# Subtracting the lower halves of the gathered expert rows on GpSimd instead of VectorE

## The chip, the cores and the metric

The kernel runs on one core of one Trainium2 chip. The metric is the device time of one launch in microseconds (us), the median of several executions. A core has a matrix engine (TensorE; PE in the profile, PEld for its weight loads), a vector engine (VectorE; DVE), an activation engine (ScalarE; ACT), GpSimd (POOL) and SyncE (SP). Each engine takes its own instructions strictly in the order in which they were written to it, and a semaphore makes an instruction wait for one of another engine or for a transfer.

## What is computed

Attention over 8 batches of 576 tokens and 8 heads, half of the heads with a local mask and half with a strided one, and then a mixture of 8 experts, each of which takes 576 of the 4608 tokens. The second half, in which the change lies, is this:

```python
def _moe_ref(x, w_gate, w1, w2):          # x: 4608 x 512, w1: 8 x 512 x 1024, w2: 8 x 1024 x 512
    logits = x @ w_gate
    ...                                    # tokens are assigned in order of their logits, 576 to an expert
    for e in range(E):
        mask = assigned == e
        h = np.maximum(x[mask] @ w1[e], 0.0)
        out[mask] = h @ w2[e]
    return out.astype(np.float32)
```

All matrices are float32. The kernel reaches that accuracy with float16 matmuls: every operand is split into an upper half (the value rounded to float16) and a lower half (value minus upper half, rounded to float16), and three of the four products are added.

## The kernel before

The attention part fills the first 200 us or so and writes the rows of x to a buffer in DRAM, `x_scr`. The experts then follow in eight rounds, numbered 0 to 7 here as `ph` is in the code. A round closes one expert. What a round does for its expert lies ahead of that expert's matmuls, beside the matmuls of the expert before it:

- A search (`search`, lines L833 to L871) finds by counting which logit is the limit for the 576 best tokens. It is a loop of VectorE, TensorE, VectorE, TensorE: `cm` (L833) compares, a matmul (L849) counts, `red` and `r` (L852, L855) reduce, a matmul (L858) sums, `g` (L865) decides, a matmul (L868) spreads it. These small matmuls stand between the large ones in TensorE's queue.
- `indices` gives the list of the expert's tokens, `idx`.
- `tokens` gathers these rows from `x_scr` with five indirect transfers issued by GpSimd (L1089, tiles `xr`; four of 128 rows and one of 64).
- `halve` turns each of the five pieces into float16 halves: ScalarE copies the upper half into `xg` (L1078), VectorE subtracts for the lower half (L1079), and SyncE issues a transposing transfer from `xg` to `xt` (L1080). There are four `xg` buffers, so that the fifth piece waits for the transpose of the first.
- `weights` loads w1 and w2 of the expert and splits them: ScalarE squares (L1011) for a scale and writes the upper halves `w1h` and `w2h` (L1029), VectorE makes the lower halves `w1l` and `w2l` (L1030).
- `ffn` does the matmuls, first the 1024 hidden rows (`hidden`, L1180, which read `xt`, `w1h` and `w1l`), then the output (L1222 for the last 64 tokens, L1228 for the others). ScalarE scales an output tile into `y` (L1238), and GpSimd scatters it with an indirect transfer (L1239).

In round 0 three of the five pieces go another way (`turn`, on TensorE), so that `halve` runs 2 + 7 x 5 = 37 times. The order of each engine is fixed when the program is built: the code above gives due times to the steps of loading, searching and halving (`T_ROWS`, `T_ROW` and others), and a priority (`urgent`) lets a step go ahead of the others on its engine. On GpSimd the experts' part holds almost nothing but the gathers and the scatters, which in each round of the middle come as five gathers and then five scatters. The matmuls of line L1180 read all 576 columns of `xt` from the second matmul on, since each weight tile meets columns 0 to 287 and then columns 288 to 575.

Of the kernel before, what the change touches and what calls it, by code (L numbers as in the profile page):

```python
# [13 lines left out]
OP = mybir.AluOpType  # L14
# [121 lines left out]
def band_stride_attention_then_capacity_moe(ctx, tc, qt, kl, ks, nl, ns, wg, w1, w2, cst, out, dbg=None):  # L136
    nc = tc.nc
# [615 lines left out]
    def urgent(ph=1):  # L753
        return tc.high_priority(offset=URGENT * (2 if ph == 0 else 1))
# [319 lines left out]
    def halve(ph, xt, xr, t, n):  # L1074
        xg = xp.tile([128, 2 * DM], F16, name="xg", bufs=4)
        xs, xv = xg[:n].rearrange("q (a j d) -> q j a d", a=2, j=2), xr[:n].rearrange("q (a d) -> q a d", a=2)
        with urgent(ph):
            nc.scalar.activation(xs[:, 0], xv, AF.Copy)  # L1078
            nc.vector.tensor_tensor(xs[:, 1], xv, xs[:, 0], op=OP.subtract)  # L1079
            nc.sync.dma_start_transpose(xt[:, :, t * 128:t * 128 + n], xg[:n])  # L1080

    def tokens(ph, idx):
        xt = xp.tile([128, 2 * 2 * 2, CAP], F16, name="xt")
        todo = []
        for t in range(NT):
            n = min(128, CAP - 128 * t)
            xr = xp.tile([128, DM], F32, name="xr", bufs=5)
            with urgent(ph):
                nc.gpsimd.indirect_dma_start(out=xr[:n], out_offset=None, in_=x_rows,  # L1089
                                             in_offset=bass.IndirectOffsetOnAxis(ap=idx[:n, t:t + 1], axis=0))  # L1090
            if ph or t >= TURNS:
                todo.append(lambda t=t, n=n, xr=xr: halve(ph, xt, xr, t, n))
            else:
                todo.append(lambda t=t, n=n, xr=xr: turn(xt, xr, t, n))
        return xt.rearrange("p (a j d) n -> p a j d n", a=2, j=2), todo
# [256 lines left out]
```

## Time and profile before

| | |
|---|---|
| median of three executions | 700.05 us (698.74 to 703.6) |
| the profiled execution | 699.79 us, its span 698.0 us |
| busy, share of the span | PE 88%, PEld 58%, DVE 66%, ACT 50%, POOL 16% |
| mean granted TensorE clock | 0.943 |
| L1079 on DVE | 37 instructions, 25.3 us in all, 689 ns mean |
| L1089 and L1239 on POOL | 40 and 40 instructions, 41.4 us and 48.2 us in all |

The profile is of one execution. Its span runs from the first instruction to the last, and about 1.8 us of the execution's time lie around it. A row of the timeline gives start, duration, engine, line, operation, output<-inputs, and in square brackets how long the engine had idled and what ended that; the start times count from the start of the span. A row of the waits names who waited, for whom, the sum in us, how many times, and the longest. A row of the chain gives a piece of the sequence of work that ended last, each step led back to what released it.

### The profile page before, as it was taken

Reading aid. Unit: us, or ns where it says so; the run is one execution under the profiler, and the core shown is the slowest. Engines: PE = TensorE matmul, PEld = TensorE weight load, DVE = VectorE, ACT = ScalarE, POOL = GpSimd, SP = SyncE. Lnnn points to the kernel's source line nnn. Section 1 sums busy time; section 2 is a strip of 40 time slices with the busy share of each in tenths; the row PEclk is TensorE's granted clock in tenths of the full one; section 3 lists DMA queues with packets and bytes.
Section 4 is the critical chain, followed back from the end, with each engine's and each line's share of the span. In section 5 each row is a group of like instructions: output and inputs, shape, how many; then the busy total and the mean of one; then the engine's idle time right before and its main releaser. Section 6 shows DMA issues by size and latency. Waiting matters only on the chain.

```text
span 698.0 us, 19758 instructions
## 1 busy us (share of the span) xinstructions
PE 614.9 (88%) x8289; PEld 407.6 (58%) x8289; DVE 460.3 (66%) x1388; ACT 348.6 (50%) x567; POOL 109.4 (16%) x124
## 2 busy tenths in 40 slices
PE   7699998989984488989989989999998998999993
PEld 4476776757764266458547547647645744755741
DVE  3767777767847778786777777778767666681200
ACT  2655754565420456582573464384375277871210
POOL 2101110111000200330240050051041032211011
PEclk9989999989975699999999999999999999999997
DMA  8958888777120630860770670491385089731010
GB/s 235 260 164 237 237 238 237 197 214 208 38 70 2 242 91 1 294 151 2 267 179 1 234 197 16 164 249 34 104 252 92 2 297 267 212 62 54 1 39 31
DMA packets 76364, 102.42 MB, mean 147 GB/s; under 512 B 41292, under 2 KB 49062, under 8 KB 75763
## 3 DMA queue, kind: packets, MB, share of 16 engines
q1 hardware_dynamic: 68195, 79.61, 40.0%
q0 software_dynamic: 7360, 21.15, 9.9%
q8 instruction: 65, 1.06, 0.7%
q10 hardware_dynamic: 720, 0.39, 0.2%
q14 instruction: 24, 0.20, 0.1%
HBM read 73.60 MB, written 18.87 MB: 132 GB/s over the span
## 4 chain that ended last, share of the span: by engine, by line
PE 20%; issue 13%; DMA 11%; DVE 10%; ACT 5%; POOL 3%; SPq 1%; POOLq 0%; ACTq 0%
PE ph L1180 16%; DMA w<-in_w_dram 6%; DMA xt<-xg 2%; DMA xr<-x_scr,idx 2%; POOL xr L1089 2%; DVE w1l L1030 2%; POOL out_dram L1239 1%; ACT jk L1011 1%; PE ph L1228 1%; DVE w2l L1030 1%; SPq L996 1%; ACT w1h L1029 1%; DVE hl L1188 1%; DVE xg L1079 1%; ACT hh L1187 1%
## 5 line engine op out<-in xcount | busy, mean ns | idle before, releaser
L1180 PE MATMUL ph<-xt,w1h 128*128 128x288 f16 (+2 forms) x1024 | 177.7, 289 | 6.2 <-DMA xt<-xg 5.1
L1180 PEld LDWEIGHTS <-w1h 128*128 128x128 f16 x1024 | 97.6, 99 | 37.6 <-issue 7.0
L1180 PE MATMUL ph<-xt,w1l 128*128 128x288 f16 (+2 forms) x512 | 111.5, 289 | 0.0
L1239 POOL DMA_INDIRECT out_dram<-y,idx x40 | 48.2, 1204 | 337.0 <-ACT y L1238 308.1
L1011 ACT ACTIVATE jk<-w 128x1024 f16<-128x1024 f32 x64 | 67.4, 1054 | 64.6 <-DMA w<-in_w_dram 63.6
L1187 ACT ACTIVATE hh<-ph 128x576 f16<-128x576 f32 (+2 forms) x72 | 42.7, 594 | 110.9 <-PE ph L1180 110.7
L1228 PE MATMUL ph<-w2h,hl 128*128 128x512 f16 x256 | 97.5, 381 | 0.0
L1228 PE MATMUL ph<-w2h,hh 128*128 128x512 f16 x256 | 97.3, 380 | 0.1
L1228 PE MATMUL ph<-w2l,hh 128*128 128x512 f16 x256 | 97.4, 380 | 0.0
L1228 PEld LDWEIGHTS <-hh 128*128 128x128 f16 x512 | 49.2, 98 | 57.9 <-issue 7.7
L1188 DVE SCALAR_TENSOR_TENSOR hl<-ph,hh 128x576 f16<-128x576 f32 (+2 forms) x72 | 49.5, 687 | 46.6 <-ACT hh L1187 46.6
L1180 PEld LDWEIGHTS <-w1l 128*128 128x128 f16 x512 | 50.5, 99 | 13.5 <-issue 0.6
L1089 POOL DMA_INDIRECT xr<-x_scr,idx x40 | 41.4, 1034 | 52.5 <-DMA w<-in_w_dram 25.5
L371 ACT ACTIVATE pr<-spa 128x576 f32<-128x576 f32 x32 | 20.8, 650 | 56.5 <-PE spa L368 45.6
L1030 DVE SCALAR_TENSOR_TENSOR w1l<-w,w_sw,w1h 128x512 f16<-128x512 f32 x64 | 45.4, 744 | 4.9 <-ACT w1h L1029 4.8
L1228 PEld LDWEIGHTS <-hl 128*128 128x128 f16 x256 | 25.0, 98 | 39.6 <-issue 14.8
L1030 DVE SCALAR_TENSOR_TENSOR w2l<-w,w_sw,w2h 128x512 f16<-128x512 f32 x64 | 46.3, 742 | 1.8 <-ACT w2h L1029 1.3
L1238 ACT ACTIVATE y<-ph,so 128x512 f32<-128x512 f32 x32 | 21.7, 680 | 45.7 <-PE ph L1228 31.8
L1029 ACT ACTIVATE w2h<-w,w_sw 128x512 f16<-128x512 f32 x64 | 41.2, 711 | 5.4 <-DVE w_sw L206 5.4
L1029 ACT ACTIVATE w1h<-w,w_sw 128x512 f16<-128x512 f32 x64 | 42.1, 708 | 3.0 <-DVE w_sw L206 1.8
L422 POOL DMA_DIRECT2D x_scr<-xs x23 | 15.0, 657 | 173.3 <-DVE xs L406 124.9
L1079 DVE TENSOR_TENSOR xg<-xr,xg 128x512 f16<-128x512 f32 (+1 forms) x37 | 25.3, 689 | 16.0 <-ACT xg L1078 15.7
(610 smaller groups left out, 973.9 us busy)
## 6 DMA issues: line engine op xcount, KB each, us to landing
w<-in_w_dram SPq DMA_DIRECT2D x64, 512.0 KB
kl<-in_kl_dram SPq DMA_DIRECT2D x16, 304.0 KB
v_s<-in_ns_dram SPq DMA_DIRECT2D x16, 292.5 KB
v_l<-in_nl_dram SPq DMA_DIRECT2D x16, 292.5 KB
ks<-in_ks_dram SPq DMA_DIRECT2D x16, 288.0 KB
qs<-in_qt_dram SPq DMA_DIRECT2D x16, 288.0 KB
ql<-in_qt_dram SPq DMA_DIRECT2D x16, 288.0 KB
x_scr<-xl SPq DMA_DIRECT2D x8, 512.0 KB
```

What stands on the lines that cost most here:

```text
L371: nc.scalar.activation(pr[:, :S].rearrange("k (h n) -> k h n", h=2), u.sp[p][:, :, :HS], AF.Exp, scale=0.125)
L1011: nc.scalar.activation(jk, wf[:, c * n4:(c + 1) * n4].rearrange("p c f -> p (c f)"), AF.Square, scale=1.41422, accum_out=sq[:, c:c + 1])
L1029: nc.scalar.activation(hi[:, c, f], wf[:, c, f], AF.Copy, scale=s_)
L1030: nc.vector.scalar_tensor_tensor(lo[:, c, f], wf[:, c, f], s_, hi[:, c, f], op0=OP.mult, op1=OP.subtract)
L1079: nc.vector.tensor_tensor(xs[:, 1], xv, xs[:, 0], op=OP.subtract)
L1089: nc.gpsimd.indirect_dma_start(out=xr[:n], out_offset=None, in_=x_rows, in_offset=bass.IndirectOffsetOnAxis(ap=idx[:n, t:t + 1], axis=0))
L1180: nc.tensor.matmul(tile_[:, j, :w], wt[:, d, f * 128:(f + 1) * 128], xt[:, d // 2, xx, d % 2, c], start=(k == 0), stop=(k == 3 * DC - 1))
L1187: nc.scalar.activation(hv, src, AF.Relu)
L1188: nc.vector.scalar_tensor_tensor(lv, src, 0.0, hv, op0=OP.max, op1=OP.subtract)
L1228: nc.tensor.matmul(py, a[:, f, ts_], w[:, f], start=(k == 0), stop=(k == len(todo) - 1))
L1238: nc.scalar.activation(y, py, AF.Copy, scale=so[:, t:t + 1])
L1239: st = nc.gpsimd.indirect_dma_start(out=out_rows, out_offset=bass.IndirectOffsetOnAxis(ap=idx[:n, t:t + 1], axis=0), in_=y[:n], in_offset= ...
```

## The change

The subtraction of `halve` moves from VectorE to GpSimd. Operands, shapes and results stay the same.

```diff
     def halve(ph, xt, xr, t, n):
         xg = xp.tile([128, 2 * DM], F16, name="xg", bufs=4)
         xs, xv = xg[:n].rearrange("q (a j d) -> q j a d", a=2, j=2), xr[:n].rearrange("q (a d) -> q a d", a=2)
         with urgent(ph):
             nc.scalar.activation(xs[:, 0], xv, AF.Copy)
-            nc.vector.tensor_tensor(xs[:, 1], xv, xs[:, 0], op=OP.subtract)
+            nc.gpsimd.tensor_tensor(xs[:, 1], xv, xs[:, 0], op=OP.subtract)
             nc.sync.dma_start_transpose(xt[:, :, t * 128:t * 128 + n], xg[:n])
```

GpSimd's queue before, in the middle rounds: the gathers of a round (L1089) and then five scatters (L1239) of the expert before.

```order
L1089 DMA xr<-x_scr,idx 128x512 x4
L1089 DMA xr<-x_scr,idx 64x512
L1239 DMA out_dram<-y,idx 4608x512 x5
L1089 DMA xr<-x_scr,idx 128x512 x4
L1089 DMA xr<-x_scr,idx 64x512
```

The same stretch of GpSimd's queue now, from the gathers of round 2 to those of round 3.

```order
L1089 DMA xr<-x_scr,idx 128x512 x4
L1089 DMA xr<-x_scr,idx 64x512
L1239 DMA out_dram<-y,idx 4608x512
L1079 TENSOR_TENSOR xg<-xr,xg 128x2x256 x4
L1239 DMA out_dram<-y,idx 4608x512
L1079 TENSOR_TENSOR xg<-xr,xg 64x2x256
L1239 DMA out_dram<-y,idx 4608x512 x3
L1089 DMA xr<-x_scr,idx 128x512 x4
L1089 DMA xr<-x_scr,idx 64x512
```

Four subtractions stand behind a scatter, and the fifth stands behind a second scatter. Round 1 has three subtractions, a scatter and then two; round 7 has all five right behind its gathers. In round 0 a library instruction of GpSimd, without a wait, stands in front of the first subtraction:

```order
L1002 MEMSET w_4214 128x6
L1079 ISA
L1079 TENSOR_TENSOR xg<-xr,xg 128x2x256
L1079 TENSOR_TENSOR xg<-xr,xg 64x2x256
L1239 DMA out_dram<-y,idx 4608x512 x2
```

VectorE's queue in round 3 (`w_6390` is that round's w1, `pr__6675` and `pr__6755` two steps of the search), with the difference marked:

```order
 L1030 SCALAR_TENSOR_TENSOR w1l<-w_6390,w_sw_6396,w1h 128x4x128 x3
-L1079 TENSOR_TENSOR xg<-xr,xg 128x2x256
 L852 TENSOR_TENSOR red<-pr__6675,fold 68x32
-L1079 TENSOR_TENSOR xg<-xr,xg 128x2x256
 L855 TENSOR_REDUCE r_6687<-red 68x8
-L1079 TENSOR_TENSOR xg<-xr,xg 128x2x256
+L1030 SCALAR_TENSOR_TENSOR w1l<-w_6390,w_sw_6396,w1h 128x4x128
 L865 TENSOR_SCALAR g_6703,ih_6704<-pr__6675 128x8
-L1079 TENSOR_TENSOR xg<-xr,xg 128x2x256
-L1030 SCALAR_TENSOR_TENSOR w1l<-w_6390,w_sw_6396,w1h 128x4x128
```

The five subtractions are gone, and one weight half has moved ahead of `g`. ScalarE's queue in the same round:

```order
-L1029 ACTIVATE w1h<-w_6390,w_sw_6396 128x4x128
-L1078 ACTIVATE xg<-xr 64x2x256
-L1238 ACTIVATE y<-ph,so 128x512
-L1029 ACTIVATE w1h<-w_6390,w_sw_6396 128x4x128 x3
+L1029 ACTIVATE w1h<-w_6390,w_sw_6396 128x4x128 x2
+L1238 ACTIVATE y<-ph,so 128x512
+L1078 ACTIVATE xg<-xr 64x2x256
+L1029 ACTIVATE w1h<-w_6390,w_sw_6396 128x4x128 x2
```

The upper half of the fifth piece now stands behind an output tile `y`. The queues of TensorE and SyncE are the same as before.

## Prediction

> **What bounds the kernel now.** I read the page's busy times first, then the table of stretches for the middle of the experts, then TensorE's waits, and then the timeline of one handover from expert to expert.
>
> ```profile
> PE 614.9 (88%) x8289; PEld 407.6 (58%) x8289; DVE 460.3 (66%) x1388; ACT 348.6 (50%) x567; POOL 109.4 (16%) x124
> ...
> 400.00:456.00 56.00, 52.65 (x433) 33.12 (x432) 41.64 (x130) 30.74 (x52) 12.60 (x10) 1.00 0.47 141
> ```
>
> The second row is a stretch of 56 us in which one round passes: TensorE is busy 52.65 us (94%), VectorE 41.64, GpSimd 12.60. TensorE is the bound, and since its order does not change, the change can only act through what TensorE waits for.
>
> ```profile
> PE ph L1180 <- DMA xt<-xg: 5.1, 3, 2.4
> ...
> PE pr__8285 L858 <- DVE r L855: 3.1, 1, 3.1
> ...
> PE pr__7520 L858 <- DVE r L855: 1.6, 1, 1.6
> ...
> PE pr__5910 L858 <- DVE r L855: 1.4, 1, 1.4
> ...
> PE pr__6755 L858 <- DVE r L855: 1.3, 1, 1.3
> ```
>
> Two kinds of wait meet at the handover. One is for a search step of VectorE (`r`), late because VectorE is full of weight halves and of the subtractions that the change takes away; these four waits, one each in rounds 5, 4, 2 and 3, make 7.4 us. The other is for the transposed rows `xt`, which come out of the subtractions: 5.1 us. So the moved instruction feeds one wait and lengthens the other, and the question is which of them ends last. In round 3 the feeding looks like this (ScalarE, VectorE, GpSimd and TensorE in turn):
>
> ```profile
> 405.70 0.62 ACT L1078 ACTIVATE xg<-xr 128x512 f16<-128x512 f32 x1
> 410.15 0.61 ACT L1078 ACTIVATE xg<-xr 128x512 f16<-128x512 f32 x1
> 412.84 0.67 ACT L1238 ACTIVATE y<-ph,so 128x512 f32<-128x512 f32 x1
> 406.36 0.69 DVE L1079 TENSOR_TENSOR xg<-xr,xg 128x512 f16<-128x512 f32 x1
> 413.19 0.68 DVE L1079 TENSOR_TENSOR xg<-xr,xg 64x512 f16<-64x512 f32 x1
> 407.46 0.91 POOL L1089 DMA_INDIRECT xr<-x_scr,idx  x1 [0.30 <-issue]
> 408.68 1.02 POOL L1239 DMA_INDIRECT out_dram<-y,idx  x1 [0.30 <-issue]
> L1180 PE MATMUL ph<-xt,w1h x4: 283/284/285, 418.4 to 418.7; 128*128 128x288 f16 x4
> ```
>
> VectorE takes up the first piece at 406.36, while GpSimd is still issuing gathers; it ends the fifth at 413.87, and TensorE needs `xt` at 418.4. How long a transpose needs is in the chain, rounds 1, 2 and 6:
>
> ```profile
> 305.24 3.78 DMA xt<-xg
> ...
> 353.28 3.63 DMA xt<-xg
> ...
> 583.43 3.42 DMA xt<-xg
> 586.86 0.05 issue
> 586.90 3.26 PE ph L1180 x16
> ...
> L1080 SPq DMA_TRANSPOSE xt<-xg x37: 1193/1302/3070, 251.9 to 612.9; - x37
> ...
> 640.67 0.97 POOL L1239 DMA_INDIRECT out_dram<-y,idx  x1 [4.16 <-ACT y L1238]
> ```
>
> From its issue to its landing 3.4 to 3.8 us pass, 3.6 in the mean. The fifth piece of round 3 thus lands near 417.5, less than 1 us before its use; in round 6 TensorE stands waiting for it until 586.90. **The rows arrive just in time or late in every round from 1 to 6**, so lateness of the subtractions has almost nothing to hide behind. Round 7 is the exception: the last transpose is issued at 612.9, and round 6's last output tile is scattered only at 640.67, so that round 7's rows lie ready some 20 us ahead.
>
> **The change part by part.**
>
> What goes from VectorE:
>
> ```profile
> L1079 DVE TENSOR_TENSOR xg<-xr,xg 128x512 f16<-128x512 f32 (+1 forms) x37 | 25.3, 689 | 16.0 <-ACT xg L1078 15.7
> L1030 DVE SCALAR_TENSOR_TENSOR w1l<-w,w_sw,w1h 128x512 f16<-128x512 f32 x64 | 45.4, 744 | 4.9 <-ACT w1h L1029 4.8
> ```
>
> 37 times 0.689 us, 25.3 us in all or 3.4 us in a round. Of this only the 7.4 us of waits above could come back, and only where `xt` is there in time; I count none of it in the sum, because the rows come later.
>
> What GpSimd gets has no row of its own: no elementwise operation with inputs runs on it in this trace. The nearest rows are its memsets.
>
> ```profile
> L245 POOL MEMSET v_s<- 128x1560 f32 x2 | 2.8, 1387 | 0.0
> L245 POOL MEMSET v_l<- 128x260 f32 x2 | 0.6, 304 | 0.0
> L1239 POOL DMA_INDIRECT out_dram<-y,idx x40 | 48.2, 1204 | 337.0 <-ACT y L1238 308.1 <-DVE red L852 16.6 <-DVE y L1236 6.2
> ```
>
> 1300 more elements cost 1083 ns, or 0.833 ns each, and some 0.09 us are left as the fixed part. One stream of 512 elements then costs 0.43 us. If the two reads and the write all overlap, a subtraction takes 0.09 + 0.43 = 0.52 us; if the three follow one another, 0.09 + 1.28 = 1.37. I take 1.2, nearer to the upper end: a memset only writes, and two reads have to be brought in besides. The 64-row pieces cost the same, as on VectorE (0.68 us at 413.19): each partition has 512 elements.
>
> The Trainium skill's page "GPSIMD Engine Reference" (section 3.1, Elementwise) speaks against the change: it puts a two-input operation there at about 2.6 cycles an element at 1.2 GHz, which gives an estimate of 1.1 us for 512 elements, and near 1.2 with a dispatch. No run here shows it yet; by 1.1 us the sum below would be 3 us smaller.
>
> Where it stands in GpSimd's queue costs more. The first four subtractions come behind the last gather and one scatter, the fifth behind another scatter (1.2 us and 0.3 of issue). These are the scatters behind the gathers in rounds 1, 2, 4, 5 and 6; round 3's is above:
>
> ```profile
> 299.81 1.23 POOL L1239 DMA_INDIRECT out_dram<-y,idx  x1 [0.30 <-issue]
> 353.23 2.30 POOL L1239 DMA_INDIRECT out_dram<-y,idx  x1 [0.30 <-ACT xg L1078]
> 464.72 1.26 POOL L1239 DMA_INDIRECT out_dram<-y,idx  x1 [0.30 <-ACT xg L1078]
> 519.74 1.02 POOL L1239 DMA_INDIRECT out_dram<-y,idx  x1 [0.30 <-issue]
> 577.55 1.05 POOL L1239 DMA_INDIRECT out_dram<-y,idx  x1 [0.30 <-issue]
> ```
>
> The last piece lands at the end S of that scatter plus five subtractions (6.0), one scatter (1.5) and one transpose (3.6), that is S + 11.1. The upper halves do not delay this: the fifth waits for the first transpose, S + 1.2 + 3.6 + 0.6 = S + 5.4, before GpSimd reaches it at S + 6.3, and the `y` that the inner scatter waits for is at hand (413.5 in round 3, against S + 4.8 = 414.5). SyncE's transposes, about 1.3 us each, keep pace with 1.2. The times at which TensorE starts L1180 in earnest:
>
> ```profile
> 309.07 0.54 PE L1180 MATMUL ph<-xt,w1h 128*128 128x288 f16 x3 [1.70 <-DMA xt<-xg]
> L1180 PE MATMUL ph<-xt,w1h x6: 282/286/296, 362.9 to 363.9; 128*128 128x288 f16 x6
> L1180 PE MATMUL ph<-xt,w1h x8: 283/286/286, 473.6 to 474.7; 128*128 128x288 f16 x8
> L1180 PE MATMUL ph<-xt,w1h x4: 402/447/448, 531.7 to 532.4; 128*128 128x288 f16 x4
> ```
>
> Round 1: 301.04 + 11.1 = 312.1 against 309.1, late by 3.1. Round 2: 355.5 + 11.1 = 366.6 against 362.9, 3.7. Round 3: 409.7 + 11.1 = 420.8 against 418.4, 2.4. Round 4: 466.0 + 11.1 = 477.1 against 473.6, 3.5. Round 5: 520.8 + 11.1 = 531.9 against 531.7, 0.2. Round 6: 578.6 + 11.1 = 589.7 against 586.9, 2.8. **Together 15.7 us.** I take a delay to stay: search, indices and gathers of the next round hang on small matmuls in TensorE's queue, so that the next round begins later by as much.
>
> Now both engines read SBUF at once during the burst of weight halves, which no row of before shows either. Between the first and the fifth subtraction of a round, VectorE has five weight halves of 0.66 us (spacing within the runs of three) and one `cm` of 0.79, all with two SBUF inputs: 4.1 us. The cost in a round lies between nothing and 4.1. I take two collisions on the path, 1.3 us, as most of the run of three can pass during the inner scatter: 6 x 1.3 = 7.9.
>
> Other parts: scatters behind the subtractions start up to 6 us later, and only ScalarE's `y` tiles wait for them, of which there are three, written about 5 us apart: nothing. The next gathers stand behind them, but are due 40 us later. ScalarE's moved piece costs nothing beyond its place, as shown. GpSimd's library instruction of round 0 lies in an idle stretch between 241.2 and the first upper half:
>
> ```profile
> 241.12 0.12 POOL L1002 MEMSET w<- 128x6 f32 x1
> L1078 ACT ACTIVATE xg<-xr x37: 613/629/630, 250.5 to 611.0; 128x512 f16<-128x512 f32 x29, 64x512 f16<-64x512 f32 x8
> ```
>
> That gap of 9 us covers it; without the cover it would cost what exceeds 9 us.
>
> **Sum:** 699.8 (the profiled execution, 0.3 below the median) + 15.7 + 7.9 = 723.4, so 723.
>
> **The rivals.**
>
> *The two engines shut each other out.* If an operation of one holds the other off for its whole length, each round pays five weight halves, 3.3 us, in place of 1.3: 699.8 + 15.7 + 19.8 = 735; with `cm` too, 740. For it: the five follow close upon one another. Against it: nothing seen yet. The Trainium skill's page "SBUF — State Buffer" (Who interferes with whom) has this rule: a VectorE instruction with two SBUF inputs and a GpSimd instruction that reads SBUF exclude each other, and the second waits for the whole of the first. No run here shows it so far.
>
> *The subtraction is cheap.* At 0.52 us and without sharing costs, a round lands at S + 7.7: 308.7, 363.2, 417.4, 473.7, 528.5, 586.3, within 1 us of need or early. Then the time stays at 699 to 702. Against it stands the price.
>
> *VectorE's relief wins*, the other side: the four waits for `r` shrink by what VectorE no longer does ahead of them, 7.4 us, and the time is 692. It decides only if `xt` lands before TensorE arrives in rounds 2 to 5, so if five subtractions plus all sharing take under about 2.5 us. GpSimd cannot start before S, while VectorE in round 3 had begun at 406.36, 3.3 us earlier; that speaks against it.
>
> **How the numbers follow.** The forecast (late rows, little sharing, 709 to 730) 0.55; shut out (730 to 745) 0.27; cheap 0.13; relief 0.05. A measurement here tells about 1% (7 us) from no change. Faster by over 1% is the relief, 0.05; within it is the cheap case and the edge of the forecast, 0.13; slower 0.82. The range reaches from 705, a subtraction at two streams (0.94 us) with little sharing, to 740, the shut-out in full.
>
> **What would show it.** Of the profile after: GpSimd about 44 us busier with 37 operations near 1.2 us, VectorE 25 us less if `w1l` keeps its 744 ns (a longer `w1l` is the shut-out); the wait of L1180 for `xt` grown from 5.1 us in three places to some 25 in six; the waits for `r` smaller or unchanged. The prediction fails if a delay in one round is made up in the next, or if a subtraction is far off 1.2 us.

## The result

The changed kernel is slower: 725.61 us median of four executions (722.02 to 729.13) against 701.83 us (698.74 to 704.39) of the kernel before; the ratio is given as 1.041, with a 95% interval of 1.036 to 1.046. The two medians themselves stand at 1.034, below that interval, and why is not known; a second comparison later gave 1.033 (1.028 to 1.038), so that the loss is best read as 3.3 to 4.1%. Here and below the ratios leave out slow executions (over 1.5% above the fastest of the same kernel), while the medians hold all. The profiled execution of the changed kernel took 722.02 us, span 720.2, mean granted clock 0.919 (before: 699.79, 698.0, 0.943). The forecast, 723 us, was met; how it came about was only partly what the prediction said.

The page's busy times of the changed kernel, and from its table of groups the subtraction, the weight halves of w1 and of w2:

```profile
PE 622.8 (86%) x8286; PEld 408.9 (57%) x8289; DVE 472.2 (66%) x1351; ACT 349.0 (48%) x567; POOL 144.1 (20%) x161
...
L1079 POOL TENSOR_TENSOR xg<-xr,xg 128x512 f16<-128x512 f32 (+1 forms) x37 | 42.2, 1168 | 9.6 <-ACT hh L1187 8.5
L1030 DVE SCALAR_TENSOR_TENSOR w1l<-w,w_sw,w1h 128x512 f16<-128x512 f32 x64 | 74.5, 1194 | 26.9 <-ACT w1h L1029 26.8
L1030 DVE SCALAR_TENSOR_TENSOR w2l<-w,w_sw,w2h 128x512 f16<-128x512 f32 x64 | 46.3, 742 | 1.7 <-ACT w2h L1029 1.5
```

The last of these groups in the kernel before:

```profile
L1030 DVE SCALAR_TENSOR_TENSOR w2l<-w,w_sw,w2h 128x512 f16<-128x512 f32 x64 | 46.3, 742 | 1.8 <-ACT w2h L1029 1.3 <-DMA xt<-xg 0.3
```

A subtraction takes 1.168 us on GpSimd, and its 37 take 42.2 us. VectorE gave up 25.3 us of subtractions and yet is 11.9 us busier (460.3 to 472.2): `w1l` grew from 45.4 us to 74.5, while `w2l`, the same operation at a time when GpSimd subtracts nothing, stayed at 742 ns. TensorE's longest waits at the handover now, from the table of its waits:

```profile
PE pr__6675 L868 <- DVE g L865: 6.6, 1, 6.6
PE pr__8205 L868 <- DVE g L865: 6.4, 1, 6.4
...
PE ph L1180 <- DMA xt<-xg: 6.0, 2, 3.8
PE pr__7440 L868 <- DVE g L865: 5.9, 1, 5.9
PE pr__5910 L868 <- DVE g L865: 5.4, 1, 5.4
...
PE pr__5227 L849 <- DVE cm L833: 2.1, 1, 2.1
...
PE pr__5227 L858 <- DVE r L855: 0.9, 1, 0.9
```

Four waits for `g` that were not there before, one in each of rounds 2 to 5, make 24.3 us. The four waits for `r` (7.4 us) are gone; the longest one left is 0.9. The wait for `xt` has hardly grown (5.1 to 6.0) and is all in round 6. In round 1 the 2.1 us for `cm` are new: there three subtractions hold `cand` for 3.67 us (0.24 otherwise). Where a wait for `g` comes from shows in the timeline of round 3: GpSimd, VectorE and TensorE in turn.

```profile
412.81 1.01 POOL L1239 DMA_INDIRECT out_dram<-y,idx  x1 [0.30 <-issue]
413.85 4.48 POOL L1079 TENSOR_TENSOR xg<-xr,xg 128x512 f16<-128x512 f32 x4
413.72 5.16 DVE L1030 SCALAR_TENSOR_TENSOR w1l<-w,w_sw,w1h 128x512 f16<-128x512 f32 x1 [3.51 <-ACT w1h L1029]
418.81 0.15 DVE L865 TENSOR_SCALAR_CACHE_REDUCE g<-pr__6675 128x8 f16<-128x8 f32 x1
419.02 0.16 PE L868 MATMUL pr__6675<-ih,ones_j 128*128 128x1 f16 x1 [6.56 <-DVE g L865]
```

One weight half, 0.74 us otherwise, lasts 5.16 us: from its start to 0.55 us after the last of four subtractions that GpSimd makes without a gap (413.85 + 4.48 = 418.33). `g` stands behind it on VectorE, and TensorE waits 6.56 us for `g`. The cost does not end there. Here are the table of stretches for some 6 us before and after TensorE's return (the granted clock is the third number from the end), and four of the matmuls after it:

```profile
412.00:419.00 7.00, 0.46 (x3) 0.10 (x1) 5.28 (x4) 4.30 (x8) 5.99 (x6) 0.81 0.70 169
419.00:425.00 6.00, 5.98 (x27) 2.49 (x27) 4.74 (x9) 2.43 (x4) 2.16 (x2) 0.65 0.57 131
...
419.43 0.64 PE L1228 MATMUL ph<-w2h,hh 128*128 128x512 f16 x1
419.86 0.64 PE L1228 MATMUL ph<-w2l,hh 128*128 128x512 f16 x1
...
423.47 0.38 PE L1228 MATMUL ph<-w2l,hh 128*128 128x512 f16 x1
423.69 0.38 PE L1228 MATMUL ph<-w2h,hl 128*128 128x512 f16 x1
```

After the idle stretch the granted clock is 0.65; matmuls follow one another every 0.43 us until about 423.2, and then every 0.22. In the 5 us behind the waits of rounds 2, 4 and 5 (from 357, 479 and 541) it is 0.52, 0.50 and 0.50. Some ten matmuls at 0.2 us more are 2 us a round on top of the wait. In the stretches that go from the first L1180 of a round to that of the next, rounds 1 and 2, before and then after:

```profile
307.10:362.90 55.80, 51.85 (x434) 33.05 (x432) 41.39 (x129) 30.24 (x50) 11.89 (x10) 1.00 0.50 144
362.90:418.40 55.50, 52.38 (x434) 32.99 (x433) 40.94 (x128) 29.91 (x50) 12.60 (x10) 1.00 0.46 139
```

```profile
306.10:366.00 59.90, 54.30 (x434) 33.77 (x433) 43.09 (x122) 30.16 (x50) 15.23 (x15) 0.93 0.42 130
366.00:427.50 61.50, 53.93 (x433) 33.49 (x432) 43.60 (x123) 30.23 (x50) 16.34 (x15) 0.94 0.41 127
```

The same 434 or 433 matmuls take 2.0 us more busy time (51.85 + 52.38 = 104.2 against 108.2, so 4.0 in two rounds) at a clock of 0.93 and 0.94 in place of 1.00, and the two rounds are 4.1 and 6.0 us longer. Over the profiled executions all waits of TensorE add up to 71.8 us before and 86.2 after, 14.4 more: `g` +23.8, `r` -9.8 (the four waits and smaller ones), `cm` +1.5, `xt` +0.9, all others -2. With the busy time (+7.9, from 614.9) that makes 22.3 us, and the spans differ by 22.2.

### The profile page after: what moved, and what is told of

It reads as the page before. It is cut to its first block, busy times and chain, and to the rows that moved or that the text cites. A ratio compares the mean times of both kernels' runs of the same rounds, so it can differ in the third digit from the quotient of the medians.

```text
span 720.2 us, 19772 instructions
## 1 busy us (share of the span) xinstructions
PE 622.8 (86%) x8286; PEld 408.9 (57%) x8289; DVE 472.2 (66%) x1351; ACT 349.0 (48%) x567; POOL 144.1 (20%) x161
## 4 chain that ended last, share of the span: by engine, by line
PE 33%; DVE 12%; DMA 11%; issue 4%; ACT 3%; POOL 2%; SPq 1%; POOLq 0%; ACTq 0%
PE ph L1180 20%; PE ph L1228 10%; DMA w<-in_w_dram 5%; DMA xr<-x_scr,idx 4%; DVE w1l L1030 3%; DVE w2l L1030 1%; DVE hl L1188 1%; ACT jk L1011 1%; DMA out_dram<-y,idx 1%; DVE cm L833 1%; PE ph L1222 1%; POOL xr L1089 1%; POOL xg L1079 1%; ACT hh L1187 1%; DVE cand L871 1%
## 5 line engine op out<-in xcount | busy, mean ns | idle before, releaser
L1180 PE MATMUL ph<-xt,w1h 128*128 128x288 f16 (+2 forms) x1024 | 177.3, 289 | 7.3 <-DMA xt<-xg 6.0
L1180 PEld LDWEIGHTS <-w1h 128*128 128x128 f16 x1024 | 97.4, 98 | 38.8 <-issue 7.1
L1180 PE MATMUL ph<-xt,w1l 128*128 128x288 f16 (+2 forms) x512 | 111.7, 289 | 0.0
L1239 POOL DMA_INDIRECT out_dram<-y,idx x40 | 40.3, 1008 | 314.1 <-ACT y L1238 284.8
L1228 PE MATMUL ph<-w2h,hl 128*128 128x512 f16 x256 | 102.2, 399 | 0.0
L1228 PE MATMUL ph<-w2h,hh 128*128 128x512 f16 x256 | 101.6, 397 | 0.0
L1228 PE MATMUL ph<-w2l,hh 128*128 128x512 f16 x256 | 101.3, 396 | 0.0
L1030 DVE SCALAR_TENSOR_TENSOR w1l<-w,w_sw,w1h 128x512 f16<-128x512 f32 x64 | 74.5, 1194 | 26.9 <-ACT w1h L1029 26.8
L1228 PEld LDWEIGHTS <-hh 128*128 128x128 f16 x512 | 50.9, 101 | 63.7 <-issue 17.3
L1180 PEld LDWEIGHTS <-w1l 128*128 128x128 f16 x512 | 50.5, 99 | 13.6 <-issue 0.7
L1089 POOL DMA_INDIRECT xr<-x_scr,idx x40 | 41.8, 1045 | 55.3 <-DVE L L937 25.4
L1079 POOL TENSOR_TENSOR xg<-xr,xg 128x512 f16<-128x512 f32 (+1 forms) x37 | 42.2, 1168 | 9.6 <-ACT hh L1187 8.5
```

The source lines that it names most:

```text
L1030: nc.vector.scalar_tensor_tensor(lo[:, c, f], wf[:, c, f], s_, hi[:, c, f], op0=OP.mult, op1=OP.subtract)
L1079: nc.gpsimd.tensor_tensor(xs[:, 1], xv, xs[:, 0], op=OP.subtract)
L1180: nc.tensor.matmul(tile_[:, j, :w], wt[:, d, f * 128:(f + 1) * 128], xt[:, d // 2, xx, d % 2, c], start=(k == 0), stop=(k == 3 * DC - 1))
L1228: nc.tensor.matmul(py, a[:, f, ts_], w[:, f], start=(k == 0), stop=(k == len(todo) - 1))
L1239: st = nc.gpsimd.indirect_dma_start(out=out_rows, out_offset=bass.IndirectOffsetOnAxis(ap=idx[:n, t:t + 1], axis=0), in_=y[:n], in_offset= ...
```

## The experiments

Two theories. **A**: GpSimd's subtractions, while they follow one another, hold off every VectorE operation that reads two tensors from SBUF; the time is lost where such an operation stands ahead of a search step. **B**: the time is lost because the pieces come late, through GpSimd's queue and its slower subtraction. Ratios are to the kernel before, with 95% intervals. The edits are shown in short; what only keeps an order is left out of them.

### GpSimd only writes

```diff
-nc.gpsimd.tensor_tensor(xs[:, 1], xv, xs[:, 0], op=OP.subtract)
+fill = nc.gpsimd.memset(gap640, 0.0), nc.gpsimd.memset(xs[:, 1], 0.0)   # both behind the ScalarE copy
```

> GpSimd holds its place and its time but reads nothing: each subtraction becomes two memsets, one of 640 and one of 512 elements, some 1.1 to 1.2 us together, behind the same ScalarE copies; the lower halves are left zero. The order of every other engine is that of the changed kernel, so the weight half still stands ahead of g. Theory A (reading subtractions on GpSimd hold VectorE's two-input operations off for as long as they follow one another): the w1l group falls from 1194 ns to about 745, the four waits for g (24.3 us) go, TensorE's clock dips at those places go too, and the time is 700 to 708; rows may be late by some us in single rounds. Theory B (the time is lost because the pieces come late through GpSimd's queue, whatever they read): the time stays within 1% of 722, and w1l stays near 1.19 us or the waits turn up at xt.

Measured: 706.46 us, 1.010 (1.002 to 1.019). The orders of the other four engines are those of the changed kernel; the memsets take 0.65 and 0.54 us, as much together as a subtraction. The group of `w1l`, the waits of TensorE, and round 3 in the timeline (the weight half that stands ahead of `g`):

```profile
L1030 DVE SCALAR_TENSOR_TENSOR w1l<-w,w_sw,w1h 128x512 f16<-128x512 f32 x64 | 46.0, 779 | 31.5 <-ACT w1h L1029 27.4 <-issue 4.1
...
PE ph L1180 <- DMA xt<-xg: 15.5, 8, 4.4
PE pr__6699 L868 <- DVE g L865: 2.1, 1, 2.1
...
410.63 0.75 DVE L1030 SCALAR_TENSOR_TENSOR w1l<-w,w_sw,w1h 128x512 f16<-128x512 f32 x1 [2.91 <-ACT w1h L1029]
410.74 0.66 POOL L1078 MEMSET gap<- 128x640 f16 x1
```

The weight half runs through at 0.75 us beside the memsets, and the longest wait for `g` is 2.1 us. **What is left, 1.0%, has two sources.** One is the later pieces: waits for `xt` of 15.5 us, 10.4 more than before. The other is `g`: in rounds 2 to 5 TensorE still waits 1.2 to 2.1 us for it, 6.7 us together, without any hold. In rounds 3 and 5 (2.1 us each) this is the place of the weight half, which waits for its upper half `w1h` with `g` behind it. Against both stands the relief of `r` (13.6 us in all before, 3.8 here). So of the 3.3 to 4.1% that the changed kernel loses, some 2.3 to 3.1% go with what GpSimd reads. A holds; B has at most a part of the smaller share.

### One SBUF input for the lower halves of w1

```diff
-nc.vector.scalar_tensor_tensor(lo, w, s_, hi, op0=OP.mult, op1=OP.subtract)
+nc.vector.tensor_scalar(lo, w, s_, 0.0, op0=OP.mult, op1=OP.max, accum_out=ac)   # for w1, behind hi as before
```

> The changed kernel, but the lower weight halves of w1 are made from one SBUF input (scale and a maximum with zero, with a running sum so that the operation stays near its length); the subtraction of the upper half is left out there. The subtractions stay on GpSimd. Theory A, with the detail that only operations with two SBUF inputs are held off: w1l falls to about 0.7 us even beside GpSimd's four subtractions, the waits for g go, and the next two-input operation in line (cand or cm) is held off instead, up to 3 to 4 us a round, which TensorE may have to wait for; time 703 to 715. If every VectorE operation were held off, one input or two, w1l stays near 1.19 us and the time near 722. Theory B: time near 722, w1l irrelevant.

Measured: 711.42 us, 1.016 (1.007 to 1.025). The subtractions on GpSimd in round 3, the weight half that starts with them, and `cand` behind it:

```profile
414.29 4.49 POOL L1079 TENSOR_TENSOR xg<-xr,xg 128x512 f16<-128x512 f32 x4
414.31 0.75 DVE L1030 TENSOR_SCALAR_CACHE_REDUCE w1l<-w,w_sw 128x512 f16<-128x512 f32 x1 [2.24 <-issue]
416.15 2.67 DVE L871 SCALAR_TENSOR_TENSOR cand<-steps,pr__6700,pre 128x18 f32<-128x18 f32 x1
```

The weight half with one SBUF tensor passes in 0.75 us in the midst of the four subtractions. `cand`, 18 elements a partition and 0.24 us otherwise, but with two tensors from SBUF, is held until 418.82, just past the end of the four at 418.78. So it is the kind of operands that counts, not the amount of data. The next operation in line is held in its place, as A said, and TensorE waits 1.3 us for the `cm` behind it; most of the excess over the writing kernel is gone. What this kernel still loses is not all hold: in rounds 2, 4 and 5 TensorE waits 3.5 us for `r`, but VectorE itself stands idle there for 3.75 to 4.36 us ahead of `red`, and the trace does not say why.

### The weight half behind `g`

```diff
 # VectorE, rounds 2 to 5; all other queues unchanged
-w1l, g, ss, cand, cm
+g, ss, cand, cm, ... w1l
```

> The changed kernel with one difference on one engine: in rounds 2 to 5 the weight half that stands ahead of g on VectorE is put behind g. All other queues are the same, and nothing is left out. If the place of that weight half in VectorE's queue is what turned the hold into lost time (theory A, order part): the four waits for g (24.3 us) go; the hold then falls on cand or cm behind g, whose users on TensorE stand some us further on, so that about half to all of the loss returns, 701 to 713, with w1l still above 0.9 us. If the hold costs the same wherever it falls (theory A without the order): waits of 3 to 5 us a round move to cand or cm, time 716 to 726. Theory B: no change, 722, or waits for xt of 10 to 16 us in place of those for g.

In the edit, `ss` (L1017) sums up the squares for a weight's scale. Measured: 713.03 us, 1.018 (1.010 to 1.027), the upper end of what A gave. The waits for `g` fall to 1.2 us at most. In round 3 the hold falls on `cand`, and TensorE waits for `cm` behind it:

```profile
412.21 4.49 POOL L1079 TENSOR_TENSOR xg<-xr,xg 128x512 f16<-128x512 f32 x4
414.09 2.64 DVE L871 SCALAR_TENSOR_TENSOR cand<-steps,pr__6675,pre 128x18 f32<-128x18 f32 x1
417.62 0.72 PE L849 MATMUL pr__6755<-ohn,cm 128*68 128x32 f16 x9 [3.44 <-DVE cm L833]
```

6.6 us of waiting have become 3.4 in that round. So about half of the loss, from 3.3 to 4.1% down to 1.8%, hangs on one row of VectorE's queue in each of four rounds; the other half does not. Part of that other half is again a wait for `r` of 3.5 us, in round 4, behind an idle VectorE (4.2 us ahead of `red`) and not behind a held one.

### A gap between the subtractions

```diff
+nc.gpsimd.memset(xs[:, 1, 0], 0.0)      # 256 elements, behind the ScalarE copy
 nc.gpsimd.tensor_tensor(xs[:, 1], xv, xs[:, 0], op=OP.subtract)
```

> The changed kernel with a memset of 256 elements (about 0.3 us, it only writes) on GpSimd ahead of the subtraction of each piece, mostly between two subtractions. If VectorE gets its turn as soon as GpSimd does something that reads nothing: the weight half of rounds 2 to 5 ends after one or two subtractions, near 1.5 to 2.7 us in place of 5.2, the waits for g fall from 5.4 to 6.6 us to 1 to 3 each, and the time is 705 to 716, although GpSimd's chain is 1.2 us longer. If GpSimd keeps its hold across the gap, or the hold is not tied to single instructions: w1l near 6 us, waits for g of 6.5 to 8 us, time 724 to 730. Theory B: 722 to 728 with the loss at xt.

Measured: 722.7 us, four executions from 713.47 to 727.26, 1.026 (1.013 to 1.039): no gain that can be told from the changed kernel, though the hold itself was broken. In rounds 2 to 6 GpSimd's order came out as two memsets, two subtractions and the same again, so that the gap lies behind every second subtraction. Round 3, GpSimd and then VectorE:

```profile
419.33 2.28 POOL L1079 TENSOR_TENSOR xg<-xr,xg 128x512 f16<-128x512 f32 x2
421.56 0.56 POOL L1078 MEMSET xg<- 128x256 f16 x2
422.08 2.54 POOL L1079 TENSOR_TENSOR xg<-xr,xg 128x512 f16<-128x512 f32 x2
420.66 1.00 DVE L871 SCALAR_TENSOR_TENSOR cand<-steps,pr__6687,pre 128x18 f32<-128x18 f32 x1
423.45 3.04 DVE L1030 SCALAR_TENSOR_TENSOR w1l<-w,w_sw,w1h 128x512 f16<-128x512 f32 x3
```

`cand` is let through at 421.66, when two subtractions have ended and a memset runs, while two more subtractions are still to come. In round 3 of the changed kernel nothing of VectorE got in between subtractions that touch. But the chain of GpSimd is longer, and the waits come back elsewhere: 14.6 us for `xt`, and waits for `r` of 3.7, 3.7, 3.5 and 3.0 us. In round 3 the weight halves that are held now (3.04 us for three) stand ahead of that `r`; in round 2 VectorE is idle ahead of it. The expectation for the time (705 to 716) failed; that for the hold was right.

### GpSimd subtracts for nobody

```diff
 nc.vector.tensor_tensor(xs[:, 1], xv, xs[:, 0], op=OP.subtract)        # as before
+nc.gpsimd.tensor_tensor(scratch, xv, xs[:, 0], op=OP.subtract)         # nobody reads it
```

> The kernel before, with VectorE still making every lower half, and besides it the same subtraction on GpSimd into a scratch tile that nobody reads. The orders of TensorE, VectorE, ScalarE and SyncE are those of before; GpSimd has its five subtractions of a round in one run, about 5.7 us. Theory A (the reading subtractions hold VectorE's two-input operations off): VectorE's own subtractions, weight halves and cand stand still for up to 5.7 us a round, rows and search come late although GpSimd makes neither, and the time is 712 to 735. Theory B (lateness of the pieces through GpSimd's queue): nothing of the path hangs on GpSimd now, so the time is that of before within 1%, 698 to 703.

Measured: 730.46 us, 1.050 (1.045 to 1.056), more than the change itself. In round 3 five subtractions stand in one run on GpSimd, and one of VectorE's own meets them:

```profile
423.22 5.59 POOL L1079 TENSOR_TENSOR lone<-xr,xg 128x512 f16<-128x512 f32 x5
423.41 5.95 DVE L1079 TENSOR_TENSOR xg<-xr,xg 128x512 f16<-128x512 f32 x1 [1.18 <-ACT xg L1078]
429.29 0.15 DVE L865 TENSOR_SCALAR_CACHE_REDUCE g<-pr__6699 128x8 f16<-128x8 f32 x1
```

An operation of 0.69 us lasts 5.95, up to 0.55 us after GpSimd's last. Rounds 2, 4, 5 and 6 show the same, with 5.2 to 6.8 us. Nothing on the path reads what GpSimd makes, so that B, which expected no change, is refuted as the main cause.

### One piece, and the rounds at the ends

```diff
-xg = xp.tile(..., bufs=4)
+xg = xp.tile(..., bufs=5)                                                       # five buffers
-nc.gpsimd.tensor_tensor(...)
+(nc.gpsimd if t == NT - 1 else nc.vector).tensor_tensor(...)                    # fifth piece alone
+(nc.gpsimd if ph in (0, E - 1) else nc.vector).tensor_tensor(...)               # rounds 0 and 7 alone
+(nc.gpsimd if ph in (0, E - 1) or t == NT - 1 else nc.vector).tensor_tensor(...) # both
```

> GpSimd subtracts only for the fifth piece of 64 rows of each round, VectorE for the other four; the orders of TensorE, ScalarE and SyncE are those of before. Theory A: one subtraction holds VectorE for at most 1.2 us and no four follow one another, so that at most 1 us a round is lost and 0.68 us of VectorE's time comes back: 697 to 705, within 1% of before; w1l near 0.76 us. Theory B: the fifth piece ends a round's rows and its place behind a scatter is what costs; most of the loss stays, 708 to 722, with waits for xt of 10 us or more.

The fifth piece alone: 694.68 us, 1.000 (0.996 to 1.003). From its table of groups:

```profile
L1030 DVE SCALAR_TENSOR_TENSOR w1l<-w,w_sw,w1h 128x512 f16<-128x512 f32 x64 | 46.6, 760 | 8.8 <-ACT w1h L1029 8.8
...
L1079 POOL TENSOR_TENSOR xg<-xr,xg 64x512 f16<-64x512 f32 x8 | 9.7, 1210 | 34.4 <-ACT xg L1078 34.4
```

A subtraction costs 1.21 us on GpSimd, and `w1l` is at 760 ns; one subtraction by itself holds VectorE too briefly to matter, and `xt` is waited for 5.1 us, as before. This piece stands behind one scatter here and waits for its upper half (L1078), not for GpSimd; in the changed kernel it stands behind two scatters, and what that place costs by itself was not tried.

> The kernel before with five buffers for the gathered halves in place of four, so that the fifth upper half need not wait for the first transpose. The prediction said that the rows come just in time or late in rounds 1 to 6. If so, the fifth piece is ready some 1 to 2 us earlier, the waits for xt (5.1 us) fall to under 2, and the time is 693 to 699. If the waits for r (7.4 us) or the gathers set the end instead, the time is that of before, 698 to 702.

Five `xg` buffers, VectorE everywhere: 699.34 us, 1.008 (1.004 to 1.011), slower, against both cases of the expectation (the kernel before stood at 694.5 in this comparison). The waits for `xt` stay (5.5 us), and TensorE's waits for `cm` grow, from the table of its waits in rounds 4, 3, 2 and 5:

```profile
PE ph L1180 <- DMA xt<-xg: 5.5, 3, 2.8
PE pr__7520 L849 <- DVE cm L833: 2.2, 1, 2.2
PE pr__6755 L849 <- DVE cm L833: 1.8, 1, 1.8
PE pr__5990 L849 <- DVE cm L833: 1.6, 1, 1.6
...
PE pr__8285 L849 <- DVE cm L833: 1.3, 1, 1.3
```

Before, no round from 1 to 6 had such a wait of 1 us or more. In VectorE's queue the fifth subtraction now stands ahead of `cand` and `cm`, for which TensorE's small matmuls wait, and a weight half has moved between these two. A fifth buffer by itself does not shorten the waits for `xt`.

> As the last one, with five buffers, and GpSimd subtracts in rounds 0 and 7 only, where in the changed kernel no weight half of the path was held off and the rows lie ready early. Theory A: no loss there, and round 0's waits for cm and r (2.8 us before, 1.4 after) shrink by 1.4: 691 to 699, 1 us under the last kernel. If GpSimd's reads cost also where VectorE has time to spare: 700 to 706.

With GpSimd in rounds 0 and 7 besides: 698.12 us, 1.000 (0.995 to 1.004), 0.8% under the last kernel. The forecast was 1 us; where the rest of the difference comes from is not shown. In round 7 a weight half lasts 4.85 us beside the five subtractions there, and TensorE does not wait for it.

> The changed kernel with GpSimd subtracting in rounds 0 and 7 only, VectorE in rounds 1 to 6, and four buffers as before. The last two kernels, with five buffers, stood at 1.008 (VectorE everywhere) and 1.000 (GpSimd in rounds 0 and 7) of before. Theory A: no weight half of the path meets a subtraction in these two rounds, and round 0 saves up to 1.4 us of waits for cm and r: 0.990 to 0.999 of before. If the difference of the last two was chance: 0.998 to 1.004.

With four buffers: 692.54 us, 0.996 (0.992 to 1.000).

> As the last one, and the fifth piece of every round on GpSimd too, which alone stood at 1.000. Theory A: one subtraction by itself costs at most 1 us a round and VectorE gets 0.68 us back; the sum of the two is within 0.4% of the last kernel, 0.990 to 1.002 of before. If the two disturb each other (a later round 1, a longer wait for r): 1.004 or more.

Both together: 693.86 us, 0.995 (0.990 to 0.999). That is below the kernel before by 0.1 to 1%, as far as the interval tells; where subtractions stand alone or in rounds with time to spare, moving them is harmless or a little better.

> The changed kernel itself once more, beside more runs of the kernel before, so that the other ratios have a firm one to stand against. The first comparison gave 1.041 (1.036 to 1.046), the medians shown with it 725.61 and 701.83, a quotient of 1.034. Theory A with the place of the weight half in the queue: 1.030 to 1.045, above the kernel with g first (1.018, 1.010 to 1.027) and the one that only writes (1.010, 1.002 to 1.019), each with its interval. If it comes out under 1.025, the place of the weight half explains nothing.

The changed kernel again: 718.99 us, 1.033 (1.028 to 1.038), with the same four waits for `g` (5.4 to 6.2 us). The intervals of the writing kernel and of the one with `g` first lie below this one.

## Why the prediction was right, and where it was not

**The price of a subtraction** was right: 1.168 us against 1.2. The estimate from the Trainium skill's page "GPSIMD Engine Reference" (section 3.1, Elementwise), 1.1 and with a dispatch near 1.2, agrees with this row. The library instruction of round 0 is hidden, as argued: GpSimd idles 8.5 us ahead of its first subtraction, until ScalarE releases it.

**The late rows, 15.7 us, are the term that failed.** In the changed kernel the waits for `xt` grew by 0.9 us. With the hold taken away, in the kernel that only writes, late rows do cost: 15.5 us in place of 5.1, so 10.4 more. In the changed kernel TensorE is itself held up, and meets the rows as they land: in rounds 2 to 5 the last transposes are issued at 362.5, 424.1, 484.3 and 546.5, and L1180 starts 3.4 to 4.0 us later, at 366.0, 427.5, 488.3 and 550.1; a transpose took 3.4 to 3.8 us before. The two delays lie beside each other; the sum added them. One step inside S + 11.1 was wrong for these rounds as well. It had the `y` of the inner scatter at hand, but that `y` comes out of the TensorE that is held up, and GpSimd idles for it. Round 3:

```profile
421.92 1.00 POOL L1239 DMA_INDIRECT out_dram<-y,idx  x1 [3.60 <-ACT y L1238]
422.95 1.16 POOL L1079 TENSOR_TENSOR xg<-xr,xg 64x512 f16<-64x512 f32 x1
```

The fifth subtraction ends at 424.11, 10.3 us behind S (413.82), where the prediction had 7.5.

**The sharing, 7.9 us, was far too small**, and its mechanism was that of the rival that had 0.27. The step "two collisions on the path, 1.3 us" a round priced a collision at the length of a weight half, 0.66 us. The weight half waits for the whole run of subtractions: it lasts 5.16 us, and TensorE waits 5.4 to 6.6 us in each of four rounds, of which 1.2 to 2.1 are left in the kernel that only writes, where nothing is held. Another 2 us a round go at a lower clock: the prediction let the change act only through what TensorE waits for, and TensorE's busy time grew by 7.9 us. The sign that the prediction had named for the shut-out, a longer `w1l`, is the one that came (1194 ns), while the wait for `xt` reached 6.0 us in two places and not some 25 in six. The order rows had shown the weight half ahead of `g`; the prediction did not ask who is queued behind it. The rival's own sum (five weight halves at 0.66 us, on top of the late rows, 735) was wrong in the same way: it counted operations, where the length of GpSimd's run sets the cost, and it added the rows.

The Trainium skill's page "SBUF — State Buffer" (Who interferes with whom) gave the rule of that rival, and the traces agree in both parts: a VectorE operation with two SBUF inputs is held off by a GpSimd operation that reads (5.16 us for 0.74), not by one that only writes (0.75 us beside a memset). They add that in rounds 2 to 5 the hold passes from one subtraction to the next when they touch: four made 4.48 us, and nothing of VectorE with two SBUF inputs got in between. That the second of the two waits, as the Trainium skill's page has it, is less plain in the records: the weight half of round 3 starts 0.13 us ahead of the first subtraction (413.72 and 413.85) and is the one that is held.

**VectorE's relief, counted as nothing,** was real: the four waits for `r`, 7.4 us, went, and smaller ones with them (9.8 us in all). In the kernel that only writes it sets off most of what the later pieces cost (`r` -9.8 us against `xt` +10.4).

Two sums beside the forecast do not follow from their own terms. The lower end of the range, 705, was given for a subtraction of 0.94 us; by the same working the rows land at S + 9.8, late by 9 us in all, and the time is 709 before any sharing. And the cheap rival's S + 7.7 leaves out that the fifth upper half is ready only at S + 0.5 + 3.6 + 0.6 = S + 4.7, so that its rows would land about 1 us later.

So 723 was met by luck, by errors that cancel: rows +15.7 in place of +1, sharing +7.9 in place of some 32 with the clock, relief 0 in place of some -10.

## What to carry to other kernels

Before an elementwise operation with SBUF inputs goes to GpSimd, look at what stands on VectorE at that time with two SBUF inputs, and who waits behind it: the cost here was mostly the length of GpSimd's unbroken run, paid by the first such operation, however small it is. Keep such operations apart or in stretches where VectorE has time, and write the order so that a short step that TensorE waits for comes ahead of the bulk. When two delays end at the same engine, take the later one, not their sum.

## What had not been expected of the hardware

The hold does not end with an instruction: four subtractions that follow without a gap held one operation 5.16 us, five 5.95 us, and a memset of 0.3 us in between let the waiting one through. There is an exception: in round 7 of the kernel that subtracts for nobody, subtractions of VectorE end between those of GpSimd (1.66 and 1.65 us each), and three of GpSimd's take 1.6 us there in place of 1.16. Why the run gives way there is open.

And a VectorE operation with one SBUF tensor and a scalar, `pre` (L841, 0.23 us otherwise), is held off too, by subtractions (2.59 us beside two of them in round 1 of the changed kernel) and by memsets as well. So theory A's rule of two SBUF tensors does not cover all that is held. From the timeline of the changed kernel, and then of the kernel that only writes:

```profile
298.94 2.59 DVE L841 TENSOR_SCALAR pre<-steps,cand 128x18 f32<-128x18 f32 x1
299.22 2.27 POOL L1079 TENSOR_TENSOR xg<-xr,xg 128x512 f16<-128x512 f32 x2
```

```profile
413.59 1.42 DVE L841 TENSOR_SCALAR pre<-steps,cand 128x18 f32<-128x18 f32 x1
413.85 0.66 POOL L1078 MEMSET gap<- 128x640 f16 x1
414.42 0.55 POOL L1078 MEMSET xg<- 128x512 f16 x1
```

Beside the memsets it ends at 415.01, and the last memset at 414.97. The Trainium skill's page "SBUF — State Buffer" (Who interferes with whom) says that a `tensor_scalar` without an accumulator can enter a mode that uses the ports it shares with GpSimd, and then contends with any GpSimd instruction; the one-input weight half, which writes an accumulator, was not held (0.75 us), which agrees. What sets `pre` apart was not tried by itself.
